# Two-layer dilated attention and GeGLU on one core: exponentials in a PSUM bank of their own, one-bank projection tiles, and a new order table

## The chip, the cores and the metric

The kernel runs on one core of a Trainium2 chip. A core has a matrix engine (TensorE, "PE" in the profile, with its weight loads shown apart as "PEld"), a vector engine (VectorE, "DVE"), a scalar engine (ScalarE, "ACT"), a general engine (GpSimd, "POOL") and an engine that here only issues transfers (SyncE, "SP"). PE writes its products into PSUM, 128 partitions of 16 KB, which this kernel cuts into eight banks of 2 KB (512 float32 columns). The metric is the device time of one execution in microseconds. The time before is the median of three runs, 1265.81 us (1263.17 to 1267.76).

## What is computed

Two layers, each an attention block and a feed-forward block, applied twice to the same weights. The attention looks back at eight positions two apart; positions of one parity see only their own parity.

```python
def _A_ref(x, wqkv, wo):                      # S=2048, D=512, H=32 heads of Dh=16
    W, dil = 8, 2
    q, k, v = split of (x @ wqkv)
    idx = pos[:, None] - (jnp.arange(W) * dil)[None, :]
    logits = einsum("bhsd,bhswd->bhsw", q, k[idx]) * Dh ** -0.5   # -1e9 where idx < 0
    attn = softmax(logits)
    return einsum("bhsw,bhswd->bhsd", attn, v[idx]).reshape(B, S, D) @ wo

def _B_ref(x, w_gate, w_up, w_down):          # F=1792
    return (gelu(x @ w_gate) * (x @ w_up)) @ w_down

x = A_x
x = x + _A_ref(layernorm(x), A_wqkv, A_wo)
x = x + _B_ref(layernorm(x), B_w_gate, B_w_up, B_w_down)
x = x + _A_ref(layernorm(x), A_wqkv, A_wo)
x = x + _B_ref(layernorm(x), B_w_gate, B_w_up, B_w_down)
```

## The kernel before

**Tiling.** The sequence is split by parity and then into chunks of 256 positions (J = 2 tiles of 128), so that a layer has eight chunks and the kernel sixteen. Every matrix is held as a high and a low float16 half, and every product is three passes (high by high, high by low, low by high) that add up in PSUM.

**Stages of a chunk.** (1) Its input is normalised, split and transposed, and projected to query, key and value: for each of the two tiles two halves of the heads, 12 products of 512 columns and 12 of 256 each (line 1047). ACT moves a half out of PSUM (line 1067, staging tile `sc`), and SP stores it to DRAM (`qkvd`). (2) SP loads the windows back (`q`, `kv`), and DVE does the attention: product (line 1131), sum over the head (1140), maximum (1162), subtraction (1167); ACT takes the exponential into PSUM (1172); DVE sums it (1177), inverts (1181), scales it in place (1186), multiplies with the values (1198) and sums (1210). This goes by two groups of heads. (3) The result `o` is split by ACT and POOL (`hl`), transposed by a transfer (`ot`), and PE multiplies it with `w_o` (line 1010 through the helper `passes`); DVE adds it to the residual `x` (1248). (4) The sum is normalised (ACT 858, POOL 934 to 948, ACT 999), split and transposed to `bx`. (5) The feed-forward runs over 14 columns of `w_g` and `w_u` in seven pairs: 48 products of 256 columns a pair (line 1010), the gelu on ACT (1302), gate times up on DVE (1310), sums of blocks on POOL (1321 to 1323), the split on ACT (1331) and POOL (1336, tiles `gh`, and the spare ends of `w_g` and `w_u`, which the profile then names), and 21 down products (line 1345) that add up in the tiles `pd` over the seven pairs. The down product is a fast one of seven blocks (numbered 1 to 7) in place of eight, put together by six DVE sums (line 1374).

**What sets the order.** Nothing is ordered by hand. `Graph.plan` runs all instructions through a list scheduler with estimated durations: of the instructions that can start soonest on an engine it takes the one with the lowest priority number. The priorities are sums of entries of the table `AT`. A tile in PSUM or SBUF is leased from a pool, and an instruction waits in the plan until a slot is free. The program is then emitted in that order, each engine works through its own queue in order, and the waits between engines are added by the tile framework when the program is built. The plan takes two pools for independent, even where their tiles lie in one bank.

**PSUM before.** Two tiles `pg` of two banks; `pds` of four, two and two blocks of 256 columns, so of two banks (profile name pd_121), one bank (pd_122) and one bank (pd_123). Block 1 of the down product is the first half of the last bank, and the exponentials `pe` (pool `P_pe`) are its second half. Until the first down product, pd_121 serves as a third `pg` and pd_122 as the tile `pt` for transposes; the lines `retire` take them away. A pair's four products (gate and up of both columns) share one two-bank `pg`, and so do a half of a projection (768 columns) and both tiles of the `w_o` product.

```python
pds = [ps.tile([P, n, HD], F32, name=f"pd{i}") for i, n in enumerate((4, 2, 2))]
P_pg = Pool("pg", [ps.tile([P, 2, 512], F32, name=f"pg{i}") for i in range(2)]
            + [pds[0].rearrange("p (b m) c -> p b (m c)", b=2)], fifo=False)
P_pe = Pool("pe", [pds[2][:, 1].rearrange("p (j h w) -> p j h w", j=JM, h=AT["ng"] * HPG)])
```

## Time and profile before

| | |
|---|---|
| median of three runs | 1265.81 us (1263.17 to 1267.76) |
| the profiled execution's own time | 1266.16 us |
| its span, first to last instruction | 1264.4 us |
| busy of the span: PE, DVE, POOL, ACT | 95%, 74%, 56%, 42% |
| mean granted PE clock | 0.986 of full |
| products on PE | 9722 |

The span is what the views of the trace describe; the execution's own time is 1.76 us longer. An engine that is busy 95% of the span leaves 62 us, and the question for each microsecond of it is what ended it. Times of the trace are counted from the span's start; "idle before" is the time an engine stood still in front of an instruction, with the instruction or transfer that ended it behind the arrow.

### The profile page before, as it was taken

What the parts mean: (1) busy time and instruction counts of PE and PEld (TensorE: products, weight loads), DVE (VectorE), ACT (ScalarE), POOL (GpSimd) and SP (SyncE); (2) the same over time, 40 slices, a digit from 0 to 9 for tenths busy, and PEclk for the clock granted to TensorE, in tenths of its full rate; (3) what the DMA queues carried; (4) which work ended last, traced back from release to release, by engine and by line L of the source; (5) the groups of instructions that cost most, each with busy time, mean ns of one, the idle gap of its engine ahead of it and who ended that gap; (6) DMA issues with size and microseconds to landing.
All of it is one profiled execution on the core that took longest, in us unless ns stands there. A gap on an engine that the chain in (4) does not pass through costs nothing.

```text
span 1264.4 us, 23933 instructions
## 1 busy us (share of the span) xinstructions
PE 1202.5 (95%) x9722; PEld 954.3 (75%) x9722; DVE 934.4 (74%) x972; ACT 535.6 (42%) x851; POOL 703.7 (56%) x839
## 2 busy tenths in 40 slices
PE   3799989999989999999999999999999999999997
PEld 1455558887878888885778868778788888788886
DVE  7999987788779697717869877676979796578121
ACT  5887633434343534423443333434343534333321
POOL 3323527556575867562285837557565646456543
PEclk7999999999999999999999999999999999999999
DMA  9886893244535434606933454352436343253100
GB/s 350 281 240 188 231 232 106 90 138 138 148 109 153 140 96 155 169 8 192 223 100 108 138 156 137 113 165 87 146 107 168 107 145 78 73 158 63 55 18 18
DMA packets 195790, 174.75 MB, mean 138 GB/s; under 512 B 101904, under 2 KB 162656, under 8 KB 195680
## 3 DMA queue, kind: packets, MB, share of 16 engines
q1 hardware_dynamic: 195680, 173.23, 47.0%
q8 instruction: 76, 1.25, 0.4%
q14 instruction: 34, 0.28, 0.1%
HBM read 115.87 MB, written 33.73 MB: 118 GB/s over the span
## 4 chain that ended last, share of the span: by engine, by line
PE 57%; DVE 13%; POOL 11%; DMA 10%; issue 4%; ACT 3%; SPq 2%; POOLq 0%; ACTq 0%; DVEq 0%
PE pg L1010 36%; PE pd L1345 14%; PE pg L1047 6%; DMA bx<-hl 3%; POOL hl L965 3%; DVE prod L1198 3%; DVE o L1210 2%; DMA ot<-hl 1%; DMA xa<-xs 1%; POOL sc L1321 1%; DVE prod L1131 1%; DVE lg L1140 1%; DMA xs<-x 1%; POOL nw L937 1%; POOL sc L1322 1%
## 5 line engine op out<-in xcount | busy, mean ns | idle before, releaser
L1010 PE MATMUL pg<-bx,w_g 128*128 128x256 f16 x2664 | 328.4, 273 | 1.1 <-DMA bx<-hl 0.7
L1010 PE MATMUL pg<-bx,w_u 128*128 128x256 f16 x2664 | 327.3, 273 | 0.0
L1010 PEld LDWEIGHTS <-w_g 128*128 128x128 f16 x2688 | 263.6, 98 | 37.9 <-DMA bx<-hl 4.7
L1010 PEld LDWEIGHTS <-w_u 128*128 128x128 f16 x2688 | 263.8, 98 | 31.3
L1047 PEld LDWEIGHTS <-ax 128*128 128x128 f16 x1536 | 150.7, 98 | 110.6 <-issue 8.0
L1047 PE MATMUL pg<-w_q,ax 128*128 128x256 f16 (+1 forms) x1320 | 222.8, 328 | 3.0 <-DMA ax<-hl 2.0
L1310 DVE SCALAR_TENSOR_TENSOR sc<-pg,small,sc 128x512 f32<-128x512 f32 (+1 forms) x127 | 85.0, 679 | 145.3 <-ACT sc L1302 139.9
L1321 POOL TENSOR_TENSOR sc<-sc 128x256 f32<-128x256 f32 x112 | 102.3, 913 | 138.3 <-DVE sc L1310 138.0
L1198 DVE TENSOR_TENSOR prod<-kv,pd 128x1024 f32<-128x1024 f32 x128 | 152.3, 1217 | 22.5 <-PE pd L1345 21.4
L1131 DVE TENSOR_TENSOR prod<-kv,q 128x2048 f32<-128x2048 f32 x64 | 160.0, 2500 | 9.6 <-DMA kv<-qkvd 7.2
L1210 DVE TENSOR_REDUCE o<-prod 128x256 f32<-128x2048 f32 x64 | 146.0, 2281 | 17.3 <-POOL hl L965 14.5
L1140 DVE TENSOR_REDUCE lg<-prod 128x128 f32<-128x2048 f32 x64 | 145.8, 2279 | 1.0
L1302 ACT ACTIVATE sc<-pg,small 128x512 f32<-128x512 f32 (+1 forms) x127 | 78.5, 631 | 122.4 <-PE pg L1010 109.6
L965 POOL TENSOR_TENSOR hl<-o,hl 128x256 f16<-128x256 f32 x64 | 44.7, 699 | 133.8 <-ACT hl L961 133.8
L1345 PE MATMUL pd<-w_d,gh 128*128 128x256 f16 x798 | 96.0, 276 | 6.6 <-ACT pd L1172 3.4
L1345 PE MATMUL pd<-w_d,w_u 128*128 128x256 f16 x777 | 92.2, 273 | 7.6 <-ACT pd L1172 6.5
L1336 POOL TENSOR_TENSOR gh<-sc,gh 128x896 f16<-128x896 f32 x38 | 79.7, 2098 | 27.5 <-ACT gh L1331 25.6
L1345 PE MATMUL pd<-w_d,w_g 128*128 128x256 f16 x777 | 91.9, 273 | 2.5 <-ACT pd L1172 2.5
L1336 POOL TENSOR_TENSOR w_g<-sc,w_g 128x896 f16<-128x896 f32 x37 | 77.3, 2088 | 29.1 <-ACT w_g L1331 28.0
L1345 PEld LDWEIGHTS <-gh 128*128 128x128 f16 x798 | 79.0, 99 | 17.9 <-issue 7.5
L1345 PEld LDWEIGHTS <-w_u 128*128 128x128 f16 x777 | 76.0, 98 | 17.7 <-issue 8.7
L1336 POOL TENSOR_TENSOR w_u<-sc,w_u 128x896 f16<-128x896 f32 x37 | 75.3, 2036 | 24.6 <-ACT w_u L1331 24.4
(126 smaller groups left out, 1381.0 us busy)
## 6 DMA issues: line engine op xcount, KB each, us to landing
kv<-qkvd SPq DMA_DIRECT2D x128, 576.0 KB, 3.7
qkvd<-sc SPq DMA_DIRECT2D x64, 384.0 KB, 3.2
q<-qkvd SPq DMA_DIRECT2D x64, 128.0 KB, 3.5
x<-in_A_x_dram SPq DMA_DIRECT2D x9, 512.0 KB, 5.9
xs<-x SPq DMA_DIRECT2D x8, 512.0 KB, 3.0
xa<-xs SPq DMA_DIRECT2D x16, 256.0 KB, 6.0
x<-xs SPq DMA_DIRECT2D x8, 512.0 KB, 4.6
xa<-in_A_x_dram SPq DMA_DIRECT2D x14, 256.0 KB, 4.7
```

Source lines behind the costliest of these rows:

```text
L965: "POOL", t_pool(n), lambda: nc.gpsimd.tensor_sub(lo(), src(), hi()),
L1010: nc.tensor.matmul(pt, a, b, start=i == 0, stop=i == n - 1)
L1047: nc.tensor.matmul(pt[:, lo:hi], a[:, i // 2, kt], part(h * KT + kt)[:, lo:hi], start=(i, kt) == (0, 0), stop=(i, kt) == (2, KT - 1),)
L1131: nc.vector.tensor_mul(prod, win, q.tile().unsqueeze(2).to_broadcast([P, J, W, P]))
L1140: lambda lgv=lgv, heads=heads: nc.vector.tensor_reduce(lgv()[:, :, heads].rearrange("p j h w -> p j w h"), prod.rearrange("p j w (h d) -> ...
L1198: nc.vector.tensor_mul(paired[:, j].rearrange("p q (h d) t -> p q t h d", d=DH), win, by.unsqueeze(4).to_broadcast([P, W // 2, 2, HPG, DH]),)
L1210: lambda o=o: nc.vector.tensor_reduce(o.tile(), paired.rearrange("p j q c t -> p j c q t"), axis=AX.XY, op=ALU.add),
L1302: lambda sel=sel, h=h, pg=pg, g_of=g_of: nc.scalar.activation(g_of()[:, sel], pg.tile()[:, sel, 0:N], AF.Gelu_apprx_tanh, scale=cst["s_gat ...
L1310: lambda sel=sel, h=h, pg=pg, g_of=g_of: nc.vector.scalar_tensor_tensor(g_of()[:, sel], pg.tile()[:, sel, JM * P : JM * P + N], cst["c_up" ...
L1321: tt(b[:, 4:6], b[:, 0:2], b[:, 3:4].to_broadcast([P, 2, P]), op=ALU.add)
L1336: lambda blocks=blocks, gh_of=gh_of: nc.gpsimd.tensor_sub(gh_of()[:, 1], blocks(), gh_of()[:, 0]),
L1345: nc.tensor.matmul(pds_[PD_AT[m][0]].tile()[:, PD_AT[m][1]], gh_of()[:, a, G_AT[m]], wd_of(u, m, b), start=u == 0 and n == 0 and PD_AT[m][ ...
```

## The change

**Banks.** The exponentials get a tile `pe` of one bank that nothing else uses. The accumulators `pds` become four one-bank tiles of two blocks (profile names pd_121 to pd_124), with blocks 4 and 3, 5 and 2, 7 and 6, and 1 alone. For the projections three one-bank `pg` tiles are left (pg_125 to pg_127). Until the first down products, three of the accumulators serve as further `pg` and the third as `pt`.

**Projections.** A half of the query, key and value projection takes two leases, one for its 512 columns and one for its 256, and ACT moves it out in two instructions (line 1076) in place of one. The `w_o` product takes a one-bank tile for each of the two tiles of the chunk. A feed-forward pair puts both its gates in one bank and both its ups in another, in the order gate, gate, up, up, where it was gate, up, gate, up; the gelu waits for the first bank only, gate times up for the gelu and the second bank.

**Down products.** The first and last pair of a chunk, whose 21 down products are placed apart, are cut into four pieces by bank and no longer into three. The six sums are the same six, in another sequence.

**Order.** Almost every entry of `AT` has a new value, and so the plan lays the whole program out anew. The number and the shapes of PE's products are the same.

```diff
-    lq0=-6564.99, lq1=-5227.41, lf0=-588.11, lo=-978.21, lf1=-509.71, ld=28.41, pq0=-2827.04, pq1=4080.31,
+    lq0=-6024.71, lq1=-3848.17, lf0=-1122.81, lo=-1504.86, lf1=-880.86, ld=-724.89, pq0=-2261.26, pq1=1109.7,
...
-PD_AT = {5: (0, 0), 4: (0, 1), 3: (0, 2), 2: (0, 3), 7: (1, 0), 6: (1, 1), 1: (2, 0)}
+PD_AT = {4: (0, 0), 3: (0, 1), 5: (1, 0), 2: (1, 1), 7: (2, 0), 6: (2, 1), 1: (3, 0)}
...
-    pds = [ps.tile([P, n, HD], F32, name=f"pd{i}") for i, n in enumerate((4, 2, 2))]
+    pds = [ps.tile([P, 2, HD], F32, name=f"pd{i}") for i in range(4)]
+    banks = lambda *ts: [t.rearrange("p m c -> p (m c)") for t in ts]
     P_pg = Pool(
-        "pg", [ps.tile([P, 2, 512], F32, name=f"pg{i}") for i in range(2)]
-        + [pds[0].rearrange("p (b m) c -> p b (m c)", b=2)], fifo=False,
+        "pg", [ps.tile([P, 512], F32, name=f"pg{i}") for i in range(3)] + banks(pds[0], pds[1], pds[3]),
+        fifo=False,
     )
-    P_pt = Pool("pt", [pds[1].rearrange("p m c -> p (m c)")], fifo=False)
+    P_pt = Pool("pt", banks(pds[2]), fifo=False)
     P_pd = [Pool(f"pd{i}", [t]) for i, t in enumerate(pds)]
-    P_pe = Pool("pe", [pds[2][:, 1].rearrange("p (j h w) -> p j h w", j=JM, h=AT["ng"] * HPG)])
+    P_pe = Pool("pe", [ps.tile([P, JM, AT["ng"] * HPG, W], F32, name="pe")])
...
-                pg, stg = Lease(P_pg), Lease(P_sc)
+                pgs, stg = [Lease(P_pg) for _ in range(2)], Lease(P_sc)
                 ax = axs[j]
                 staged = lambda stg=stg: stg.tile()[:, 0 : 3 * HH * P]
 
-                def project(ps, h=h, pg=pg, ax=ax):
-                    pt = pg.tile().rearrange("p b c -> p (b c)")
+                cuts = ((0, 512), (512, 768))
+
+                def project(ps, cs, h=h, pgs=pgs, ax=ax):
                     a = ax.tile()
-                    for lo, hi in ((0, 512), (512, 768)):
+                    for n in cs:
+                        lo, hi = cuts[n]
                         for i, kt in ps:
                             part = w_q.lo if i == 1 else w_q.hi
                             nc.tensor.matmul(
-                                pt[:, lo:hi], a[:, i // 2, kt], part(h * KT + kt)[:, lo:hi],
+                                pgs[n].tile()[:, 0 : hi - lo], a[:, i // 2, kt], part(h * KT + kt)[:, lo:hi],
                                 start=(i, kt) == (0, 0), stop=(i, kt) == (2, KT - 1),
                             )
...
+                if l + c + j == 0:
+                    parts = [([p], (n,)) for p in every for n in range(2)]
+                else:
+                    parts = [(every, (n,)) for n in range(2)]
+                for k, (ps, cs) in enumerate(parts):
...
+                        r=[(ax, 0), *need], w=[(pgs[n], 0) for n in cs],
+                        get=[pgs[n] for n in cs] if ps[0] == (0, 0) else [],
+                        prio=prio + AT["proj"] + AT["half"] * h + AT["row"] * j + 0.01 * k, urgent=len(ps) == 1,
...
-                g.add(
-                    "ACT", t_act(768),
-                    lambda pg=pg, staged=staged: nc.scalar.activation(
-                        staged(),
-                        pg.tile().rearrange("p b c -> p (b c)")[:, 0:768],
-                        AF.Copy, scale=2.0**LQ,
-                    ),
-                    r=[(pg, 0)], w=[(stg, 0)], get=[stg], prio=prio - 3000,
-                )
+                for n, (lo, hi) in enumerate(cuts):
+                    g.add(
+                        "ACT", t_act(hi - lo),
+                        lambda n=n, lo=lo, hi=hi, pgs=pgs, staged=staged: nc.scalar.activation(
+                            staged()[:, lo:hi], pgs[n].tile()[:, 0 : hi - lo], AF.Copy, scale=2.0**LQ,
+                        ),
+                        r=[(pgs[n], 0)], w=[(stg, n)], get=[] if n else [stg], prio=prio - 3000,
...
+        for j in range(J):
+            pw = Lease(P_pg)
...
+                "PE", 12 * t_mm(512), project,
+                r=[*((ot, hg) for hg in range(HG)), *(("o", k) for k in range(KT))], w=[(pw, 0)],
+                get=[pw], prio=T - 200,
...
-            pg, gt, gh = Lease(P_pg), Lease(P_sc), Lease(P_gh)
+            pgs, gt, gh = [Lease(P_pg) for _ in range(2)], Lease(P_sc), Lease(P_gh)
             g_of = lambda gt=gt: gt.tile()[:, 0 : 2 * N].rearrange("p (f n) -> p f n", f=2)
             blocks = lambda gt=gt: gt.tile().rearrange("p (m c) -> p m c", m=7)
             gh_of = lambda gh=gh: gh.tile().rearrange("p (a m c) -> p a m c", a=2, m=7)
             fs = (2 * u, 2 * u + 1)
             hs = sorted({f // FH for f in fs})
-            weights = [(key, h * KT + k) for key in "gu" for h in hs for k in range(KT)]
-
-            def gate_up(pg=pg, fs=fs):
-                b = bx.tile()[:, 0:J]
-                for i, f in enumerate(fs):
-                    for n, w in enumerate((w_g, w_u)):
-                        pt = pg.tile()[:, i, n * JM * P : n * JM * P + N]
+
+            for n, (key, w) in enumerate((("g", w_g), ("u", w_u))):
+                def columns(pg=pgs[n], fs=fs, w=w):
+                    b = bx.tile()[:, 0:J]
+                    for i, f in enumerate(fs):
                         passes(
-                            pt.rearrange("p (j c) -> p j c", j=J),
+                            pg.tile()[:, i * N : (i + 1) * N].rearrange("p (j c) -> p j c", j=J),
                             [(wf_of(w, kt, f, True), b[:, :, 0, kt]) for kt in range(KT)]
                             + [(wf_of(w, kt, f, True), b[:, :, 1, kt]) for kt in range(KT)]
                             + [(wf_of(w, kt, f, False), b[:, :, 0, kt]) for kt in range(KT)],
                         )
 
-            g.add(
-                "PE", 48 * max(t_mm(N), 0.06), gate_up, r=[*((bx, j) for j in range(J)), *weights],
-                w=[(pg, 0)], get=[pg], prio=T + AT["gu"] * J * u,
-            )
-            gate = lambda i, pg=pg: pg.tile()[:, i, 0:N]
-            up = lambda i, pg=pg: pg.tile()[:, i, JM * P : JM * P + N]
+                g.add(
+                    "PE", 24 * t_mm(N), columns,
+                    r=[*((bx, j) for j in range(J)), *((key, h * KT + k) for h in hs for k in range(KT))],
+                    w=[(pgs[n], 0)], get=[pgs[n]], prio=T + AT["gu"] * J * u + 0.01 * n,
+                )
+            part = lambda n, sel, pgs=pgs: pgs[n].tile().rearrange("p (f c) -> p f c", f=2)[:, sel]
             both = fs[0] // FH == fs[1] // FH
             ev = T - 3000 + u
             for i in [None] if both else [0, 1]:
...
                 n = N * (2 if both else 1)
                 g.add(
                     "ACT", t_act(n, 1),
-                    lambda sel=sel, h=h, pg=pg, g_of=g_of: nc.scalar.activation(
-                        g_of()[:, sel], pg.tile()[:, sel, 0:N], AF.Gelu_apprx_tanh,
-                        scale=cst["s_gate", h],
+                    lambda sel=sel, h=h, part=part, g_of=g_of: nc.scalar.activation(
+                        g_of()[:, sel], part(0, sel), AF.Gelu_apprx_tanh, scale=cst["s_gate", h],
                     ),
-                    r=[(pg, 0), ("c_f", h)], w=[(gt, i)], get=[] if i else [gt, gh] if hold else [gt], prio=ev, table="gelu",
+                    r=[(pgs[0], 0), ("c_f", h)], w=[(gt, i)], get=[] if i else [gt, gh] if hold else [gt], prio=ev, table="gelu",
                 )
                 g.add(
                     "DVE", t_dvp(n),
-                    lambda sel=sel, h=h, pg=pg, g_of=g_of: nc.vector.scalar_tensor_tensor(
-                        g_of()[:, sel], pg.tile()[:, sel, JM * P : JM * P + N],
-                        cst["c_up", h], g_of()[:, sel], op0=ALU.mult, op1=ALU.mult,
+                    lambda sel=sel, h=h, part=part, g_of=g_of: nc.vector.scalar_tensor_tensor(
+                        g_of()[:, sel], part(1, sel), cst["c_up", h], g_of()[:, sel], op0=ALU.mult, op1=ALU.mult,
                     ),
-                    r=[(pg, 0)], w=[(gt, i)], prio=ev,
+                    r=[(pgs[1], 0)], w=[(gt, i)], prio=ev,
...
-            order = [5, 4, 3, 2, 7, 6, 1]
+            order = [4, 3, 5, 2, 7, 6, 1]
             lag = AT["late_end"] if last else AT["late"]
-            for ms in [order[:4], order[4:6], order[6:]] if u in (0, NU - 1) else [order]:
+            for ms in [order[k : k + 2] for k in range(0, 7, 2)] if u in (0, NU - 1) else [order]:
                 i = PD_AT[ms[0]][0]
...
-            step = b - a
-            return t[:, a : b + 1 : step] if step else t[:, a : a + 1].to_broadcast([P, 2, HD])
+            r = t[:, a]
+            return bass.AP(r.tensor, r.offset, [r.ap[0], [(b - a) * HD, 2], [1, HD]])
 
         parts = lambda: xl.tile()[:, 0:J].rearrange("p j (d c) -> p (j d) c", d=2)
         for to, of, sign in (
-            ((1, 2), (5, 4), 1), ((0, 3), (4, 3), 1), ((0, 3), (5, 2), -1), ((1, 2), (3, 2), 1),
+            ((0, 3), (4, 3), 1), ((2, 1), (4, 3), 1), ((1, 2), (5, 2), 1), ((0, 3), (5, 2), -1),
...
-    for q, i in ((P_pg, 2), (P_pt, 0)):
+    for q, i in ((P_pg, 3), (P_pg, 4), (P_pt, 0), (P_pg, 5)):
...
-    retire[1].order.extend(turns)
+    retire[2].order.extend(turns)
```

Three places show what moves. The first is PE at the down products of the last pair of chunk 0 (`gh` is the split tile of the pair, with PE's waits in brackets). Before, they follow two whole pairs of the next chunk:

```order
L1010 MATMUL pg_125<-bx_95,w_u 128x256
...
L1345 MATMUL pd_121<-w_d,gh 128x256
...
L1345 LDWEIGHTS gh [waits Pool_49]
...
L1345 MATMUL pd_122<-w_d,gh 128x256
...
L1345 MATMUL pd_123<-w_d,gh 128x256 [waits Activation_49]
...
L1345 LDWEIGHTS w_g
```

In the changed kernel:

```order
L1011 MATMUL pg_127<-bx_96,w_g 128x256
L1346 LDWEIGHTS gh [waits Activation_49]
L1346 MATMUL pd_121<-w_d,gh 128x256
...
L1346 LDWEIGHTS gh [waits Pool_49]
...
L1346 MATMUL pd_122<-w_d,gh 128x256
...
L1346 MATMUL pd_123<-w_d,gh 128x256
...
L1346 MATMUL pd_124<-w_d,gh 128x256
...
L1011 MATMUL pg_126<-bx_96,w_g 128x256 [waits DVE_49]
```

The product into the last bank loses its wait for ACT (pd_123 before held block 1 and the exponentials; pd_124 holds block 1 alone), and the down products stand between the gates and the ups of another pair. Over the whole program 62 down products into pd_123 carry a wait for ACT or DVE before; of the changed kernel's 2352 down products two carry a wait on the product itself, one for DVE and one for a transfer.

The second is DVE where chunk 0 adds its `w_o` product to the residual `x_91`, ahead of the first feed-forward. Before:

```order
L1131 TENSOR_TENSOR prod<-kv_104,q_107 128x2048
L730 TENSOR_TENSOR w_d<-bx_96,w_d 128x7x128
L1140 TENSOR_REDUCE lg_108<-prod 128x2x8x8
L1248 SCALAR_TENSOR_TENSOR x_91<-pd_121,small,x_91 128x512 x2
L730 TENSOR_TENSOR w_d<-sc_100,w_d 128x7x128
```

In the changed kernel:

```order
L1254 SCALAR_TENSOR_TENSOR x_91<-pd_121,small,x_91 128x512
L731 TENSOR_TENSOR w_d<-bx_96,w_d 128x7x128
L1254 SCALAR_TENSOR_TENSOR x_91<-pg_126,small,x_91 128x512
L731 TENSOR_TENSOR w_d<-sc_102,w_d 128x7x128
L1138 TENSOR_TENSOR prod<-kv_104,q_107 128x2048
L1147 TENSOR_REDUCE lg_108<-prod 128x2x8x8
```

The two additions now stand ahead of one attention product and one reduction of the next chunk, and each has a tile of its own. On PE the `w_o` product of chunk 0 moves the other way: 27 of the 32 projection halves of layer 0 stand ahead of it before, 28 in the changed kernel; in both all 32 stand ahead of the first gate.

The third is SP at the two transposes that bring the normalised chunk 0 to `bx_95`. Before:

```order
L1078 DMA qkvd_64<-sc_100 128x6x128
L970 DMA_TRANSPOSE bx_95<-hl_98 128x8x128
L970 DMA_TRANSPOSE bx_95<-hl_99 128x8x128
L1078 DMA qkvd_64<-sc_102 128x6x128
L1108 DMA q_107<-qkvd_64 128x256
```

In the changed kernel:

```order
L1115 DMA kv_104<-qkvd_64 128x1152
L971 DMA_TRANSPOSE bx_95<-hl_99 128x8x128
L1085 DMA qkvd_64<-sc_101 128x6x128
L971 DMA_TRANSPOSE bx_95<-hl_98 128x8x128
L1085 DMA qkvd_64<-sc_100 128x6x128
```

The second transpose now stands behind a store of a projection half, which waits for both of ACT's moves of that half.

49 lines of the change are left out of this document (20 added, 29 removed).

## The prediction

> **What bounds the kernel now.** I read the page's busy times first, then the waits of PE, then PE's timeline at the longest of them, then the waits of DVE.
>
> ```profile
> span 1264.4 us, 23933 instructions
> PE 1202.5 (95%) x9722; PEld 954.3 (75%) x9722; DVE 934.4 (74%) x972; ACT 535.6 (42%) x851; POOL 703.7 (56%) x839
> ```
>
> PE is busy 95% of the span, and it is the bound. What it must do follows from the time of its groups when nothing stops them:
>
> ```profile
> 944.89 3.90 PE pg L1047 x24
> ...
> 1214.93 20.96 PE pg L1010 x192
> ...
> 1243.42 12.79 PE pd L1345 x117
> ```
>
> In the chain that ended last, the second and third row give 0.109 us for 256 columns, the first 3.90 us for half a projection. So the 112 pairs take 112 x 5.24 = 587 us, the 112 groups of 21 down products 112 x 2.29 = 257, the 64 projection halves 250, the 16 `w_o` products (24 of 512 columns, 5.24 us) 84: 1178 us. That floor is the same in the changed kernel. Of it 130 us (32 halves and one `w_o`) stand ahead of the first gate in both orders, 1048 us behind it.
>
> ```profile
> 183.49 1.95 PE L1010 MATMUL pd<-bx,w_g 128*128 128x256 f16 x12 [3.46 <-DMA bx<-hl]
> ...
> 1256.23 4.37 DVE L1374 SCALAR_TENSOR_TENSOR x<-pd,small,x 128x512 f32<-128x512 f32 x6 [11.25 <-PE pd L1345]
> ```
>
> The first gate starts at 183.5, so unhindered PE would end at 1231.5; it ends at about 1256.2, and the last sums and the store take the remaining 8.2 us. The 24.7 us between are waits and a slow clock. These are the waits of PE behind 180 us:
>
> ```profile
> PE pd L1345 <- ACT pd L1172: 12.4, 10, 3.5
> ...
> PE pd L1345 <- DVE prod L1198: 4.4, 4, 1.9
> ...
> PE pd L1010 <- DMA bx<-hl: 3.5, 1, 3.5
> ...
> PE pg L1047 <- ACT sc L1067: 1.0, 1, 1.0
> ...
> PE pg L1010 <- DMA bx<-hl: 0.7, 1, 0.7
> ...
> PE pg L1010 <- DVE sc L1310: 0.3, 1, 0.3
> ```
>
> 16.8 of the 22.3 us are one thing: a down product (L1345) waits for an exponential (L1172) or for a product that reads the exponentials (L1198). No data goes from either to a down product. What they have in common is the bank pd_123. PE's timeline shows it:
>
> ```profile
> 251.25 2.13 PE L1345 MATMUL pd<-w_d,gh 128*128 128x256 f16 x18
> 255.91 0.75 PE L1345 MATMUL pd<-w_d,gh 128*128 128x256 f16 x3 [2.54 <-ACT pd L1172]
> 256.45 2.77 PE L1010 MATMUL pg<-bx,w_g 128*128 128x256 f16 x12
> ...
> 371.92 0.70 PE L1345 MATMUL pd<-w_d,w_u 128*128 128x256 f16 x3 [3.46 <-ACT pd L1172]
> ```
>
> Eighteen of the 21 products run, the three of block 1 wait. The gates behind them then take 2.77 us where twelve take 1.31. The windows name the cause:
>
> ```profile
> 180.00:200.00 20.00, 16.55 (x138) 14.12 (x137) 15.32 (x14) 8.49 (x11) 5.49 (x7) 0.91 0.64 168
> 240.00:260.00 20.00, 17.46 (x146) 14.88 (x144) 19.13 (x19) 6.58 (x9) 12.21 (x14) 0.91 0.35 110
> 360.00:380.00 20.00, 16.54 (x130) 13.38 (x128) 13.36 (x14) 9.65 (x15) 13.77 (x17) 0.91 0.35 100
> ```
>
> In the three stretches with PE's longest waits (3.46, 2.54, 3.46 us) the granted clock is 0.91, which is 20 x 0.09 = 1.8 us lost in each. The same bank holds DVE up too:
>
> ```profile
> DVE mx L1177 <- PE pd L1345: 29.5, 10, 7.7
> ...
> DVE prod L1198 <- PE pd L1345: 21.4, 13, 3.7
> ...
> DVE pd L1186 <- PE pd L1345: 5.8, 5, 1.9
> ```
>
> That is 56.7 us in which the softmax stands behind down products it has nothing to do with. So the 24.7 us behind the first gate are accounted for: 18.8 of waits (22.3 without the gate's own 3.5) and 3 x 1.8 of clock.
>
> **The change part by part.**
>
> *A bank for the exponentials.* In the changed order none of the softmax instructions waits for PE, and a down product has a wait of its own twice. So the 16.8 us go, and with two of the three long waits two clock losses, 2 x 1.8 = 3.6. DVE's 56.7 us are not added: they only keep the chain of attention from taking over. What is late next on PE is the data: `bx` and the lower halves of `gh`, below. The Trainium skill, "TensorE: Matmul & The Clock Gate", section "HAM oscillation — how this bites in real kernels", warns of idle gaps of PE above about 3.4 us. By it the 2.54 us gap would have kept the clock, and this term would be 1.8 instead of 3.6; the window 240 to 260 shows the loss, so the trace differs.
>
> *The first gate.* Chunk 0 goes from `w_o` to `bx` by a chain that PE waits for:
>
> ```profile
> 155.19 5.34 PE L1010 MATMUL pd<-w_o,ot 128*128 128x512 f16 x24
> 161.12 1.40 DVE L1248 SCALAR_TENSOR_TENSOR x<-pd,small,x 128x512 f32<-128x512 f32 x2
> ...
> 175.27 5.93 SPq L970 DMA_TRANSPOSE bx<-hl  x2
> ```
>
> The changed order has one more projection half ahead of `w_o`, so it starts 3.9 us later, at 159.1. DVE comes 4.6 us earlier (one product and one reduction are moved behind), and waits. Its second addition can start when PE is done, 164.4, and ends at 165.2, against 162.5: 2.7 us later, and `bx` and the first gate with it, while PE's own work ahead ends where it did. On SP the second transpose now stands behind a store, behind which the attention's loads are queued too; the store needs a half that PE ends at about 176.1, so the transpose could go out at 178 and not 176.9, which lies inside the 2.7. I take 2.7; the lower bound is 0, since two DVE splits are moved behind those of `w_q`, for which PE waits early on, and the upper 5, where both delays add and a little more:
>
> ```profile
> PE pd L1047 <- DVE w_q L524: 3.0, 2, 2.6
> ```
>
> *More and smaller moves by ACT.*
>
> ```profile
> L1067 ACT ACTIVATE sc<-pg 128x768 f32<-128x768 f32 x55 | 44.3, 806 | 53.6 <-PE pg L1047 38.2 <-DMA qkvd<-sc 10.6 <-POOL w_g L1336 2.0
> ...
> L858 ACT ACTIVATE sc<-x 128x512 f32<-128x512 f32 x32 | 20.1, 628 | 33.5 <-DVE x L1248 21.1 <-issue 4.3 <-POOL w_u L1336 3.8
> ...
> L1172 ACT ACTIVATE pd<-lg 128x256 f32<-128x256 f32 x8 | 3.1, 388 | 2.7 <-DVE prod L1198 2.6
> ```
>
> 512 and 256 columns take 628 + 388 = 1016 ns where 768 took 806: 64 x 0.21 = 13.4 us more on ACT. It is busy 42%, and a bank that was due in 3.9 us still is; cost 0. Without that cover the halves ahead of the first gate would bring 32 x 0.21 = 6.7 us.
>
> *Three banks for the rotation.* A gate's or up's bank is due again after two other banks, 5.24 us of products, if nothing stands between; that was so with two tiles of a pair. But in the changed order 66 of 172 such returns come after no more than these 5.24 us, before 11 of 80. And the down products stand nearer to their pair: at least 6.9 us of products behind its last up, and 13 of 112 no more than 9.5; before at least 10.5. What must fit in is gate times up, three sums, the split and its lower half:
>
> ```profile
> L1310 DVE SCALAR_TENSOR_TENSOR sc<-pg,small,sc 128x512 f32<-128x512 f32 x95 | 70.9, 746 | 117.9 <-ACT sc L1302 112.4 <-POOL nw L941 5.0
> ...
> L1321 POOL TENSOR_TENSOR sc<-sc 128x256 f32<-128x256 f32 x112 | 102.3, 913 | 138.3 <-DVE sc L1310 138.0
> L1323 POOL TENSOR_TENSOR sc<-sc 128x256 f32<-128x256 f32 x112 | 83.6, 747 | 8.8
> L1336 POOL TENSOR_TENSOR gh<-sc,gh 128x896 f16<-128x896 f32 x38 | 79.7, 2098 | 27.5 <-ACT gh L1331 25.6 <-ACT nw L867 1.7
> ```
>
> With some 0.6 us for the middle sum and 0.9 for the split that is 6.0 us when nobody is held up (the gelu is done by then, it waits for the gates alone). DVE carries instructions of 2.3 to 2.5 us and POOL of 2.1, so a chain can come late. Bounds: 0, and all 66 returns late by half a microsecond, 33. The nearest rows are the 1.3 us that PE waited for a `pg` before; the places with no slack are six times as many, which gives 8, and the gelu starts earlier: I take 6.
>
> *The tail.* The first two sums need six products and not twelve: 6 x 0.109 = 0.65 us sooner.
>
> *Sum.* 1264.4 - 16.8 - 3.6 + 2.7 + 6 - 0.65 = 1252 us of span. The profiled execution's own time, 1266.16, is 1.76 longer than its span and 0.35 above the median of the runs, so the run is 1252 + 1.4 = **1253.5**, 12 us or 1.0% less than 1265.81.
>
> **The rivals.**
>
> *The attention sets the pace of layer 0.* Until 473 us, when its sixth chunk is through, DVE feeds PE with little to spare:
>
> ```profile
> 184.00:473.00 289.00, 279.24 (x2353) 232.40 (x2352) 227.90 (x212) 117.25 (x186) 183.18 (x210) 0.98 0.44 127
> ```
> ```profile
> DVE mx L1177 <- PE pd L1345: 15.4, 4, 7.7
> ...
> DVE prod L1198 <- PE pd L1345: 4.3, 4, 1.5
> DVE pd L1186 <- PE pd L1345: 3.0, 3, 1.4
> ```
> ```profile
> 398.79 2.29 DVE L1210 TENSOR_REDUCE o<-prod 128x256 f32<-128x2048 f32 x1
> ...
> 410.43 1.89 PE L1010 MATMUL pg<-w_o,ot 128*128 128x512 f16 x8
> ```
>  If chunks come no sooner, what PE saves there (2.54 + 3.46 of the timeline, 2.7 in two shorter waits, 3.6 of clock, together 12.3) comes back as waits for `ot`, and 8.1 remain: 1264.4 - 8.1 + 2.7 - 0.65 + 1.4, about 1260. For it: DVE is busy 79% there (227.9 of 289), and PE takes a chunk's `w_o` 9.3 us after DVE's last reduction, with a split, a transpose and their queues in between. Against: DVE itself waits 22.7 us for PE's down products in the same stretch, and is relieved of it. Chance 0.17.
>
> *The change gives back what it takes.* The waits go, and PE waits for banks: each of the 66 tight returns late by 0.3 us makes 20, on the 1246 of the sum without new waits. About 1267, no change. For it: the count of tight returns. Against: 1.3 us in all before, and the gelu and gate times up now each wait for less. Chance 0.12.
>
> *Slower: the lower halves come late.* The 13 down products at 9.5 us or less have 3.5 us of room over the bare chain. One long DVE instruction ahead (2.3 us) fits in, two (4.8) do not, and POOL's own 2.1 on top makes a lag of 3.4 us. Nine of the 13 so late are 31 us: 1246 + 31 + 1.4, about 1278. It decides from the point at which the queues ahead of the chain hold more than 3.5 us at most of these places. For it: the 79% of DVE above. Against: before, no down product waited for POOL at all. Chance 0.13.
>
> **How the numbers follow.** Forecast 0.58, the rivals 0.17, 0.12 and 0.13. A measurement of this kernel tells a difference from none at about 0.3%, 3.8 us: below 1262.0 is faster, above 1269.6 slower. Forecast and first rival lie below (0.75), the second within, the third above; 0.01 of the first rival, which ends near the edge, goes to no change, and 0.02 of the second, where banks are later still, to slower. The forecast's own range is 1243 to 1262: no new wait, none of the 2 us of small ones kept and the first gate at 183.5 on the one side, 12 us of new waits and the gate 5 late on the other. It is widened to 1268 to hold the second rival, and down to 1239 for a first gate that gains its 3.46 us of waiting.
>
> **What would show it.** The waits of PE would hold no line of L1346 for the exponential (L1179) or its reader (L1205), and those of DVE none of L1184 for PE; the windows after 240 us no clock of 0.91. The first gate would stand at 186. New lines of PE behind 190 us, for `pg` or the lower halves, would sum to some 6 us. The prediction is wrong if those lines exceed 15 us, or if `w_o` waits for `ot` in the first six chunks.

## The result, and the profile after

The changed kernel takes 1246.2 us, the median of four runs (1244.98 to 1248.89), against 1265.95 in four runs of the kernel before (1263.17 to 1267.76): a ratio of 0.9849, with a 95% interval of 0.9825 to 0.9873. The forecast was 1253.5, so the direction and the mechanism held and the gain is 7.3 us larger. The profiled execution took 1246.04 us, its span 1244.3.

The page's busy times:

```profile
PE 1200.8 (97%) x9722; PEld 954.1 (77%) x9722; DVE 935.5 (75%) x972; ACT 542.0 (44%) x911; POOL 690.2 (55%) x839
```

PE does the same 9722 products in the same busy time within 2 us; of the 62 us it did not work, 43.5 are left. The chain of work that ended last, by engine, is now 84% PE (it was 57% PE, 13% DVE, 11% POOL and 10% DMA before).

The waits of PE from the first gate on (engine, line waited in, what it waited for; total us, times, longest), all of them:

```profile
PE pg L1011 <- DMA bx<-hl: 5.1, 2, 4.6
PE pg L1050 <- ACT sc L1076: 1.4, 1, 1.4
PE pg L1011 <- DMA ot<-hl: 0.5, 2, 0.3
```

No down product (L1346) waits for anything. Behind the first gate, whose own wait is 4.58, four waits of together 2.4 us are left of 17 of 18.8. PE's timeline at the first gate, and at its last group of down products:

```profile
186.11 4.45 PE L1011 MATMUL pg<-bx,w_g 128*128 128x256 f16 x24 [4.58 <-DMA bx<-hl]
190.39 2.78 PE L1011 MATMUL pd<-bx,w_u 128*128 128x256 f16 x24
...
1234.97 2.46 PE L1346 MATMUL pd<-w_d,gh 128*128 128x256 f16 x21
```

The first 24 products take 4.45 us, the next 24 2.78: one clock loss of 1.67 us is left, behind the first gate. The windows at the places of the other two (us, busy us and count of each engine, then granted clock) are back at full clock:

```profile
180.00:200.00 20.00, 15.42 (x126) 12.92 (x125) 18.25 (x18) 8.12 (x11) 6.64 (x6) 0.91 0.70 192
240.00:260.00 20.00, 20.00 (x186) 17.94 (x184) 18.39 (x18) 7.16 (x9) 9.85 (x9) 1.00 0.36 114
360.00:380.00 20.00, 20.00 (x174) 16.77 (x173) 11.88 (x12) 3.65 (x6) 8.14 (x11) 1.00 0.36 107
```

The waits of DVE, and its longest group in the kernel before:

```profile
DVE sc L1312 <- PE pg L1011: 143.1, 53, 6.9
...
DVE mx L1184 <- ACT pe L1179: 16.1, 12, 4.5
```
```profile
DVE sc L1310 <- ACT sc L1302: 143.1, 53, 11.4
```

The softmax waits for ACT's exponential alone and no longer for PE. Gate times up (L1310, now L1312) used to wait 143.1 us for the gelu, and now waits as long for the ups themselves: the gelu, which needs the gates alone, is mostly done when the ups arrive (10.6 us of waits for it are left).

**Where the time came from.** The last group of down products of the kernel before, in PE's timeline:

```profile
1254.72 2.46 PE L1345 MATMUL pd<-w_d,gh 128*128 128x256 f16 x21
```

From the first gate to the start of that group it was 1254.72 - 183.49 = 1071.2 us, and is 1234.97 - 186.11 = 1048.9, so 22.4 less. Second profiles of both kernels, shown below, give 1071.0 and 1049.9, so 21.1 less.

In the first pair the waits give 18.8 - 2.4 = 16.4. Two clock losses give 3.3: in the kernel before, 27 products from 255.91 on take 4.61 us where 0.109 each is 2.95, and 45 from 371.92 on take 6.58 where it is 4.91, so 1.67 us for each. The remaining 2 us are the stops themselves. In the prediction's rows 18 products take 2.13 us, which is 18 x 0.109 and 0.16 more: the last product before a stop is counted in full, although the next one would have started behind it after 0.109. So each stop costs 0.16 us beyond the idle time the profile shows, and 13 stops fewer are 2.1. The sum is 21.8, and 0.6 of the 22.4 stays open. In the second pair the waits give 18.7 - 3.2 = 15.5, the clock 3.3 and 15 stops fewer 2.4, together 21.2.

PE's busy time agrees: between these marks it falls from 1052.1 to 1046.4 us in the first pair. The page's total hides this, because ahead of the first gate it rises there from 147.9 to 151.9 us; in the second pair that part is 150.4 and 150.0, so the rise is not in both pairs.

### The profile page after: what moved, and what is told of

Read it like the earlier page. It is cut to its first block, busy times and chain, and to the rows that moved or that the text cites. A ratio compares the mean times of both kernels' runs of the same rounds, so it can differ in the third digit from the quotient of the medians.

```text
span 1244.3 us, 24043 instructions
## 1 busy us (share of the span) xinstructions
PE 1200.8 (97%) x9722; PEld 954.1 (77%) x9722; DVE 935.5 (75%) x972; ACT 542.0 (44%) x911; POOL 690.2 (55%) x839
## 4 chain that ended last, share of the span: by engine, by line
PE 84%; DMA 5%; DVE 4%; POOL 3%; issue 2%; ACT 1%; SPq 0%; POOLq 0%; DVEq 0%; ACTq 0%
PE pg L1011 51%; PE pd L1346 20%; PE pg L1050 9%; PE pd L1050 3%; DMA ax<-hl 2%; POOL hl L966 1%; DMA bx<-hl 1%; DMA xa<-xs 1%; DMA ot<-hl 1%; PE pd L1011 1%; DMA kv<-qkvd 1%; DVE prod L1138 1%; DMA w_d<-in_A_wqkv_dram 1%; POOL nw L938 0%; DVE w_q L525 0%
## 5 line engine op out<-in xcount | busy, mean ns | idle before, releaser
L1011 PE MATMUL pg<-bx,w_g 128*128 128x256 f16 x2664 | 310.6, 273 | 5.1 <-DMA bx<-hl 5.1
L1011 PE MATMUL pg<-bx,w_u 128*128 128x256 f16 x2664 | 309.0, 273 | 0.0
L1011 PEld LDWEIGHTS <-w_u 128*128 128x128 f16 x2688 | 263.0, 98 | 30.6
L1050 PE MATMUL pg<-w_q,ax 128*128 128x512 f16 (+1 forms) x1152 | 203.0, 334 | 6.3 <-DVE w_q L525 4.2
L1312 DVE SCALAR_TENSOR_TENSOR sc<-pg,small,sc 128x512 f32<-128x512 f32 (+1 forms) x127 | 85.1, 680 | 157.7 <-PE pg L1011 143.1
L1322 POOL TENSOR_TENSOR sc<-sc 128x256 f32<-128x256 f32 x112 | 100.4, 896 | 127.0 <-DVE sc L1312 120.9
L1138 DVE TENSOR_TENSOR prod<-kv,q 128x2048 f32<-128x2048 f32 x64 | 152.6, 2385 | 7.8 <-DMA kv<-qkvd 7.1
L1205 DVE TENSOR_TENSOR prod<-kv,pe 128x1024 f32<-128x1024 f32 x128 | 152.6, 1216 | 1.4
L966 POOL TENSOR_TENSOR hl<-o,hl 128x256 f16<-128x256 f32 x64 | 59.2, 926 | 109.9 <-ACT hl L962 109.5
L1375 DVE SCALAR_TENSOR_TENSOR x<-pd,small,x 128x512 f32<-128x512 f32 x96 | 70.5, 743 | 32.9 <-PE pd L1346 31.4
L1346 PE MATMUL pd<-w_d,gh 128*128 128x256 f16 x798 | 93.5, 273 | 0.0
L1337 POOL TENSOR_TENSOR gh<-sc,gh 128x896 f16<-128x896 f32 x38 | 76.1, 2003 | 29.8 <-ACT gh L1332 29.6
L1346 PE MATMUL pd<-w_d,w_u 128*128 128x256 f16 x777 | 91.0, 273 | 0.0
L1346 PE MATMUL pd<-w_d,w_g 128*128 128x256 f16 x777 | 90.9, 273 | 0.0
L1324 POOL TENSOR_TENSOR sc<-sc 128x256 f32<-128x256 f32 x112 | 83.6, 747 | 8.8
```

Of the source, the lines that this page charges most:

```text
L1011: nc.tensor.matmul(pt, a, b, start=i == 0, stop=i == n - 1)
L1050: nc.tensor.matmul(pgs[n].tile()[:, 0 : hi - lo], a[:, i // 2, kt], part(h * KT + kt)[:, lo:hi], start=(i, kt) == (0, 0), stop=(i, kt) == ...
L1138: nc.vector.tensor_mul(prod, win, q.tile().unsqueeze(2).to_broadcast([P, J, W, P]))
L1205: nc.vector.tensor_mul(paired[:, j].rearrange("p q (h d) t -> p q t h d", d=DH), win, by.unsqueeze(4).to_broadcast([P, W // 2, 2, HPG, DH]),)
L1312: lambda sel=sel, h=h, part=part, g_of=g_of: nc.vector.scalar_tensor_tensor(g_of()[:, sel], part(1, sel), cst["c_up", h], g_of()[:, sel], ...
L1322: tt(b[:, 4:6], b[:, 0:2], b[:, 3:4].to_broadcast([P, 2, P]), op=ALU.add)
```

## The experiments

Each ratio below is to runs of the kernel before on the same chip; their medians lay between 1265.05 and 1267.5 us.

**1. The shared bank alone put back.** Tiles, split moves and order are the changed kernel's; the exponentials lie beside block 1 again.

```diff
-        "pg", [... for i in range(3)] + banks(pds[0], pds[1], pds[3]),
+        "pg", [... for i in range(3)] + banks(pds[0], pds[1]) + [ps.tile([P, 512], F32, name="spare")],
-    P_pe = Pool("pe", [ps.tile([P, JM, AT["ng"] * HPG, W], F32, name="pe")])
+    P_pe = Pool("pe", [pds[3][:, 1].rearrange("p (j h w) -> p j h w", j=JM, h=AT["ng"] * HPG)])
```

> The changed kernel with one thing put back: the exponentials lie again in the second half of a bank, beside block 1 of the down product (pd_124); the bank that this frees serves as a startup tile. The order of all instructions is that of the changed kernel. Theory (the shared bank is what cost PE time): waits of the down products for the exponential (L1179) or its readers (L1205) come back, and DVE's waits in the softmax for down products too; 15 to 25 us slower than the changed kernel, 1261 to 1271 us. Rival (the new order is what gained, the bank is incidental): within 4 us of the changed kernel, 1243 to 1250, since the new order would keep the two users of the bank apart.

Measured: 1263.65 us median of 10 runs; to the kernel before (1266.95) a ratio of 0.9981 [0.9965, 0.9997]. Against the changed kernel's 0.9849 this is 1.3% or some 17 us slower, and nearly all of the gain is gone. Its waits of PE behind the first gate, and two of DVE's:

```profile
PE pd L1346 <- DVE prod L1205: 9.3, 10, 1.5
PE pg L1011 <- DMA bx<-hl: 4.0, 3, 1.7
...
PE pd L1346 <- ACT pd L1179: 0.8, 1, 0.8
```
```profile
DVE prod L1205 <- PE pd L1346: 14.9, 13, 3.4
DVE pd L1193 <- PE pd L1346: 12.3, 7, 3.8
```

The theory holds: the false waits are back in both directions. Directly they are 10.1 us on PE; a further 5.6 us above the 2.4 of the changed kernel are waits for `bx`, `ot`, a gelu and a lower half that come late, which fits a DVE that is held up, though no chain from one to the other was followed. All waits behind the first gate sum to 18.1 us in 19 stops, so 15.7 us and 15 stops (2.4 us) more than after. From the first gate to the last down group this kernel takes 1252.20 - 184.53 = 1067.7 us, 18.3 more than the 1049.4 of the changed kernel's two profiles, which is 15.7 + 2.4 and little else.

The new order lessens the sharing but does not evade it. For the softmax PE waits 10.1 us here against 16.8 in the kernel before, never longer than 1.5 us, and from 190 to 1240 us the granted clock is 1.00. So part of those waits and both clock losses of the kernel before go with the new order and tiles already, and the rest of this run's price is late data and stops.

**2 and 3. The two order tables exchanged.** The changed kernel with the table `AT` of before, and the kernel before with the table of the changed one.

```diff
-    lq0=-6024.71, lq1=-3848.17, lf0=-1122.81, lo=-1504.86, lf1=-880.86, ld=-724.89, pq0=-2261.26, pq1=1109.7,
+    lq0=-6564.99, lq1=-5227.41, lf0=-588.11, lo=-978.21, lf1=-509.71, ld=28.41, pq0=-2827.04, pq1=4080.31,
...
```

> The changed kernel with the order table of before: banks, tiles and split moves are new, the numbers that set the order are old. Theory (the banks are what gained): no wait of a down product for the softmax, so most of the gain stays; the table was not made for one-bank tiles, so some waits for pg or for the lower halves of gh: 1246 to 1256 us. Rival (the table is what gained): 1262 us or more.

> The kernel before with the order table of the changed kernel: shared bank and two-bank tiles as before. Theory (the banks are what gained): waits of the down products for the softmax stay at 15 us or more, 1262 to 1280 us. Rival (the table is what gained): 1244 to 1254 us.

Measured: the new banks with the old table 1309.13 us, a ratio of 1.0344 [1.0327, 1.0361]; the old banks with the new table 1270.28, 1.0042 [1.0027, 1.0056]. For the first, the expectation that most of the gain stays was wrong: it is 63 us slower than the changed kernel. The time lies in the rival's range (1262 us or more), but the second run shows that the table alone is not what gained either. The waits of PE in the first run, from 180 us on, the longest groups:

```profile
PE pg L1011 <- DMA bx<-hl: 21.5, 4, 11.3
PE pg L1011 <- ACT sc L1305: 10.3, 14, 2.1
PE pg L1011 <- DMA ot<-hl: 5.7, 5, 2.0
PE pd L1346 <- POOL gh L1337: 3.8, 3, 1.6
PE pg L1011 <- DVE sc L1312: 3.1, 4, 1.4
PE pg L1050 <- ACT sc L1305: 3.0, 1, 3.0
PE pg L1050 <- ACT sc L1076: 1.8, 4, 0.8
PE pg L1011 <- DVE x L1254: 1.5, 3, 0.8
```

Here is the rotation's price that the prediction feared: 19.7 us of waits for a bank that ACT or DVE has not yet emptied (row 2 and the last four), and chunks whose input comes up to 11.3 us late. With a table laid out for three one-bank tiles the same tiles cost 1.4 us.

The second run's time lies where it was expected, but not for the reason given: its down products wait 9.6 us for the softmax (the two rows below and 1.1 for the maximum), and not 15 or more. Its first gate, its last down group, and these waits:

```profile
198.52 2.72 PE L1010 MATMUL pg<-bx,w_g 128*128 128x256 f16 x12 [8.10 <-DMA bx<-hl]
...
1257.79 2.46 PE L1345 MATMUL pd<-w_d,gh 128*128 128x256 f16 x21
```
```profile
PE pd L1345 <- DVE prod L1198: 5.0, 7, 1.5
PE pd L1345 <- ACT pd L1172: 3.5, 4, 1.4
```

Between those marks it takes 1059.3 us, some 12 less than the kernel before, but its first gate stands 10 to 15 us later than in that kernel's two profiles (183.49 and 188.28). So the new table gains behind the first gate with the old banks too and loses as much ahead of it, which the time alone hides. Against this run the changed kernel is 9.9 us shorter behind the first gate (1059.3 less 1049.4) and reaches it 12 to 14 us sooner. Why the startup is so late with the old banks was not followed, and it is one profile.

So the bank and the table are not two gains that add up. With the new table the own bank is worth some 17 us; with the old one the new banks lose 42.

**4. The exponentials out of PSUM, order as before.** The kernel before, its order kept on every engine, with the exponentials in 1 KB of SBUF that the zeros and the identity of the start leave free.

```diff
-    ident = sb.tile([P, P], F32, name="ident")
+    ident = (pes := sb.tile([P, 2 * P], F32, name="pe"))[:, P:]
-    P_pe = Pool("pe", [pds[2][:, 1].rearrange("p (j h w) -> p j h w", j=JM, h=AT["ng"] * HPG)])
+    P_pe = Pool("pe", [pes.rearrange("p (j h w) -> p j h w", j=JM, h=AT["ng"] * HPG)])
-    zeros = sb.tile([P, P], F32, name="zeros")
+    zeros = pes[:, 0:P]
```

> The kernel before with the exponentials in SBUF (in 1 KB that the zeros and the identity matrix of the start leave free), nothing else: same order on every engine, two-bank tiles, one move per projection half. Theory: PE loses the 16.8 us of bank waits and two of three clock losses, 3.6 us, and what it meets instead is at most 3 us: 1245 to 1250 us, as fast as the changed kernel, so that tiles, split and table add nothing. Rival one (attention sets the pace of layer 0): some 8 us come off and the rest comes back as waits of w_o for ot before 473 us, 1256 to 1261 us. Rival two (the table is needed): 1262 us or more.

Measured: 1290.43 us, a ratio of 1.0195 [1.0171, 1.0220], slower than every expectation. As a test of the shared bank it fails, because it changes something else. Groups of DVE and POOL in this kernel (line, operation, tiles, count, busy us, mean ns of one, idle before):

```profile
L1198 DVE TENSOR_TENSOR prod<-kv,pe 128x1024 f32<-128x1024 f32 x128 | 201.3, 1602 | 1.1
...
L1321 POOL TENSOR_TENSOR sc<-sc 128x256 f32<-128x256 f32 x112 | 123.4, 1102 | 94.1 <-DVE sc L1310 94.0
```

and the first in the kernel before:

```profile
L1198 DVE TENSOR_TENSOR prod<-kv,pd 128x1024 f32<-128x1024 f32 x128 | 152.3, 1217 | 22.5 <-PE pd L1345 21.4
```

The waits for PE are gone (21.4 to nothing), but the product of values and exponentials takes 1602 ns and not 1217, and POOL's first sum 1102 and not 913. DVE is busy 994.6 us and not 934.4, POOL 778.1 and not 703.7. The Trainium skill, "SBUF — State Buffer", section "SBUF: two separate sides", says that a DVE instruction with two SBUF inputs and a GpSimd instruction that reads SBUF exclude each other on a port pair. The trace agrees: both engines lengthen when the second input leaves PSUM, and in the rows below where they meet. They do not show the port itself. DVE's timeline of this kernel, and POOL's beside it:

```profile
511.71 1.23 DVE L1198 TENSOR_TENSOR prod<-kv,pe 128x1024 f32<-128x1024 f32 x1
...
517.09 4.47 DVE L1198 TENSOR_TENSOR prod<-kv,pe 128x1024 f32<-128x1024 f32 x2
```
```profile
513.68 1.64 POOL L1321 TENSOR_TENSOR sc<-sc 128x256 f32<-128x256 f32 x1 [4.24 <-DVE sc L1310]
...
517.61 2.86 POOL L1336 TENSOR_TENSOR w_g<-sc,w_g 128x896 f16<-128x896 f32 x1
```

While POOL stands idle the product takes 1.23 us, as it did with PSUM; beside POOL's split two of them take 4.47. POOL's sum, which has a median of 0.73 us, takes 1.64 where it starts just after such a product (one runs from 513.51 to 514.73). Over the whole run the product takes 1204 ns at the least and 2932 at the most, and 1186 to 1251 in the kernel before.

DVE is now busy 77% of the span, and what PE waits for most is:

```profile
PE pg L1010 <- DVE sc L1310: 7.5, 6, 2.2
PE pg L1010 <- DMA ot<-hl: 7.0, 8, 1.4
```

These are late attention (`ot`, eight times) and late gate times up. It is not the prediction's first rival, which has attention set the pace up to 473 us: of the 7.0 us for `ot` 0.7 lie there, and the rest behind 700 us. The bank of its own has to be a PSUM bank, and the eight banks of the kernel before were all taken: the two-bank tiles had to go for it.

**5. ACT's split doubled.** Each of the two moves of a projection half becomes two.

```diff
-nc.scalar.activation(staged()[:, lo:hi], pgs[n].tile()[:, 0 : hi - lo], AF.Copy, scale=2.0**LQ)
+[nc.scalar.activation(
+    staged()[:, lo + c : lo + c + (hi - lo) // 2], pgs[n].tile()[:, c : c + (hi - lo) // 2], AF.Copy, scale=2.0**LQ,
+) for c in (0, (hi - lo) // 2)][-1]
```

> The changed kernel with each of ACT's two moves of a projection half cut into two again (four moves a half, 128 instructions more on ACT), order otherwise the same. Theory (ACT is far from the bound, so that the split costs nothing): ACT's busy time rises by 20 to 30 us, the time stays within 2 us of the changed kernel, 1244 to 1249. Rival (each move holds a bank that PE waits for): at least the 32 halves ahead of the first gate show it, 6 us or more, 1252 or above.

Measured: 1246.5 us, 0.9849 [0.9820, 0.9877], the same ratio as the changed kernel. ACT's busy time rises by 7.3 us (549.3 against 542.0) and not by the 20 to 30 expected, since a move of half the columns is that much shorter: two of 256 columns take 2 x 381 ns where one of 512 took 594, two of 128 take 2 x 279 for 381. The test is so a weak one, but hardly any of the 7.3 us reaches PE, whose one wait for such a move goes from 1.4 to 1.9 us. That agrees with the prediction's cost of 0 for the first split.

**6 and 7. How much room the banks have.** Each gelu done twice, then four times.

```diff
-nc.scalar.activation(g_of()[:, sel], part(0, sel), AF.Gelu_apprx_tanh, scale=cst["s_gate", h])
+[nc.scalar.activation(g_of()[:, sel], part(0, sel), AF.Gelu_apprx_tanh, scale=cst["s_gate", h]) for _ in range(2)][-1]
```

> The changed kernel with each gelu done twice (the same result is written again; 127 instructions and 79 us more on ACT), so that each gate's bank and all that follows it in the pair comes 0.63 us later. Theory (the new waits were small because the banks and lower halves have room of a microsecond or more nearly everywhere): waits of PE for pg and gh grow by 1 to 6 us, 1247 to 1253 us. Rival (the 66 returns of a bank after 5.24 us of products have no room, and the new order only just fits): two thirds of 66 x 0.63 and more, 1270 us or above.

> As the last, with each gelu done four times: 1.9 us later in each pair, ACT busy some 63%. Theory (room of some 3 us between a gate's bank and its next use): the room is used up at the tight places, PE's waits for pg and for the lower halves grow to 15 to 60 us, 1260 to 1305 us; each further microsecond of delay costs more than the first. Rival one (no room at all): 66 x 1.9 and more, 1370 us or above. Rival two (room of several microseconds): under 1256 us.

Measured: twice 1249.3 us (0.9870 [0.9840, 0.9900]), four times 1299.55 (1.0266 [1.0234, 1.0298]). PE's waits behind the first gate with two, and with four (there without two rows of 1.9 and 1.1 us for ACT):

```profile
PE pg L1011 <- DMA bx<-hl: 1.7, 2, 1.2
PE pg L1050 <- ACT sc L1076: 1.6, 1, 1.6
PE pd L1346 <- POOL w_g L1337: 0.7, 1, 0.7
PE pg L1011 <- DMA ot<-hl: 0.3, 1, 0.3
```
```profile
PE pg L1011 <- ACT sc L1305: 16.9, 10, 3.6
PE pg L1011 <- DMA ot<-hl: 8.5, 6, 3.4
PE pg L1011 <- DMA bx<-hl: 5.8, 3, 2.9
PE pd L1346 <- POOL gh L1337: 5.0, 5, 1.6
...
PE pd L1346 <- POOL w_g L1337: 1.6, 1, 1.6
...
PE pd L1346 <- POOL w_u L1337: 0.9, 2, 0.5
```

With 0.63 us more in each pair PE waits 4.3 us in place of 2.4, and nowhere for a gate's bank. With 1.9 us more it waits 41.7, ten times and 16.9 us for a gate's bank, eight times and 7.5 us for a lower half. So the gates' banks have more than 0.6 us of room everywhere, and at some ten places less than the later gelu takes; the count of tight returns told where the edge is, not how far away. That a gelu holds ACT from its other work too (`ot` and `bx` are late) is part of the second figure, and the two are not told apart.

**8 and 9. The wait of the first gate filled.** First the last projection piece ahead of the gate is computed four times; then, in its place, 36 products that nobody uses follow it, in the first gate's bank.

```diff
+                    made.append(cs)
-                    for n in cs:
+                    for n in cs * (4 if len(made) == 108 else 1):
```
```diff
-                def columns(pg=pgs[n], fs=fs, w=w):
+                def columns(pg=pgs[n], fs=fs, w=w, fill=36 * (l + c + u + n == 0)):
...
+                    for _ in range(fill):
+                        nc.tensor.matmul(pg.tile()[:, 0:N], ident16, w_o.hi(0)[:, 0:N], start=True, stop=True)
```

> The changed kernel with the last 12 projection products ahead of the first gate computed four times in place of once (36 products of 256 columns more, 3.9 us, the last result counts), so that PE's wait of 4.58 us for bx shrinks to about 0.7 us; order otherwise the same. Theory (the half clock behind a long wait of PE comes from the wait): the first gate stays at 186 us, its 24 products take 2.8 us in place of 4.45, the clock of 180 to 200 us rises from 0.91 to 1.0, and the end comes 1.7 us earlier: 1243 to 1246 us. Rival (the slow products behind a wait have another cause, such as the data or the weights of the new stage): 24 products stay at 4.4 us, and the time at 1246 or up to 1 us above.

> The changed kernel with 36 products of 256 columns (3.9 us) whose result nobody uses, put into the bank of the first gate just ahead of it, behind the last projection half; order otherwise the same. In the run with the last half computed four times the clock held, but that half's store and the next chunk's attention came 3.9 us later and PE waited 3.3 us more for bx, ot and DVE behind the first gate. Theory (those waits came from the late half, and the clock from the idle time): first gate at 186 us, 24 products in 2.8 us, waits behind it back at some 2.5 us, span 1242 to 1243.5 us, 1.7 us less than the changed kernel, time 1243 to 1246. Rival (an earlier PE meets late data anyway): clock 1.0, but the waits behind the first gate grow by 1.7 us and the span stays at 1244 us or above.

Measured: 1246.67 us (0.9849 [0.9826, 0.9872]) and 1245.95 (0.9841 [0.9819, 0.9862]). PE's timeline at the first gate, of the second of the two:

```profile
179.89 4.09 PE L1284 MATMUL pg<-w_o,ident 128*128 128x256 f16 x36
184.40 2.79 PE L1011 MATMUL pg<-bx,w_g 128*128 128x256 f16 x24 [0.42 <-DMA bx<-hl]
```

The 24 products take 2.79 us and not 4.45, and in the first kernel 2.78: the slow products come with PE's idle time, and not from the data or the weights. The time does not follow. Behind the gate PE then waits 5.7 us in the first kernel and 4.1 in the second, 2.4 before the fill and 3.2 in the second profile of the changed kernel. A saving of 1.7 us and a return of about one lie inside the spread of the runs, so whether the fill gains anything is not settled; neither kernel is measurably faster than the changed one.

**10 and 11. Both kernels again.**

> The changed kernel itself, for a second profile and for times beside the run above: 1244 to 1249 us, the first gate at 185 to 187 us, waits of PE behind it of 2 to 4 us, as in the first profile.

> The kernel before itself, for a second profile. If the first gate's place differs from run to run by as much as between the two profiles of the changed kernel (184.31 and 186.11 us), it will stand anywhere from 182 to 186 us here, and the 2.6 us between the first two profiles is partly chance; if it is fixed by the order, it stands within 0.5 us of 183.5. The waits of down products for the softmax: 15 to 19 us in 12 to 16 waits, as in the first profile; time 1263 to 1270 us.

Measured: the changed kernel 1245.36 us in five runs beside 1267.5 (ratio 0.9832 [0.9815, 0.9850]); the kernel before in its one profiled run 1270.77. The expectations missed in part: the changed kernel's first gate comes earlier than 185, and that of the kernel before at 188.28, outside both ranges given for it; its down products wait 14.9 us for the softmax in 14 waits, just under the 15 to 19, and its one time lies just above 1270. The first gate and the last group of down products in these profiles, of the kernel before and then of the changed kernel:

```profile
188.28 2.72 PE L1010 MATMUL pd<-bx,w_g 128*128 128x256 f16 x12 [4.68 <-DMA bx<-hl]
...
1259.32 2.46 PE L1345 MATMUL pd<-w_d,gh 128*128 128x256 f16 x21
```
```profile
184.31 4.45 PE L1011 MATMUL pg<-bx,w_g 128*128 128x256 f16 x24 [4.68 <-DMA bx<-hl]
...
1234.22 2.46 PE L1346 MATMUL pd<-w_d,gh 128*128 128x256 f16 x21
```

The place of the first gate is not set by the order alone: one program has it at 183.49 and 188.28, the other at 186.11 and 184.31. Four experiments that keep the changed kernel's order ahead of the gate (1, 5, 6 and 7) have it at 184.53, 185.34, 185.18 and 185.96. From the gate to the last down group the second profiles agree with the first (1259.32 - 188.28 = 1071.0, and 1234.22 - 184.31 = 1049.9), so the spread arises in the startup and the gain behind it.

## Why the prediction was right, and where its sizes were off

| term of the sum | predicted, us | measured, us |
|---|---|---|
| waits of down products for the softmax | -16.8 | -16.8 |
| two clock losses | -3.6 | -3.3 |
| first gate | +2.7 | no shift that stands out of the spread of 4.8 |
| small waits kept and new ones | 2.0 kept + 6 | 2.4 together |
| overhead of 13 stops | not in the sum | -2.1 |
| tail | -0.65 | -0.4 |
| ACT's split, on PE | 0 | 0 |

**The bank.** Right, and the first experiment shows it as the cause: with everything else new, sharing the bank again costs some 17 us. But the prediction put all of the 16.8 us and both clock losses down to the bank. With the bank shared and the new table PE waits only 10.1 us for the softmax in the new tiles and 9.6 in the old, and neither loses the clock anywhere behind the slow products of its first gate; so some 7 us of the waits and the 3.3 of clock would have gone with the order alone. What makes the bank worth 17 us all the same is late data and stops beside those 10 us, and the sum held neither. The prediction gave DVE's side no worth in time; with the bank shared, 5.6 of PE's 18.1 us are waits for late data and not for the bank, so that side may have been worth something in the new order.

**The new waits** are the term that was mis-sized, by 5.6 us (8 expected with the small ones, 2.4 found) and most of the 7.3 by which the forecast was too slow. The step at fault is "the places with no slack are six times as many, which gives 8": it multiplied a price by a count of places, 66 of 172 returns against 11 of 80, and took "after no more than 5.24 us of products" for "with no slack". The twofold gelu shows room of more than 0.6 us at all the gates' banks; the ups' banks, which DVE empties, it need not have delayed. The rows of DVE fit that: gate times up seldom stands behind a gelu now, so that a bank is emptied within some 0.7 us (the mean of L1312 is 680 ns) of its last product when DVE stands ready. The fear itself was sound. With the old table the same tiles cost 19.7 us.

**The clock.** Right in mechanism, shown by the two fills, and nearly in size: 1.67 us for each loss and not 1.8. That a wait of 2.54 us loses the clock was read rightly from the window, though not every such wait does.

**The first gate.** The step compared one profile with an order, and its figure cannot be confirmed: 183.5 was the early end of what that program does, since its second profile has 188.28. The forecast for the place, 186, lies among the values seen for the changed order (184.31 to 186.11), but that it did so is partly luck.

**The stops** were missed. Some 2 us went into "busy" in the kernel before, so that a sum over idle times alone is too small by 0.16 us a stop. The prediction's account of the 24.7 us behind the first gate closed without them (18.8 of waits and 5.4 of clock) because it took 1256.2 us for PE's end; the last down group, 2.46 us from 1254.72 on, ends at 1257.2.

**The rivals.** The attention does not set the pace of layer 0: PE waits for `ot` 0.5 us in all. Even with 60 us more on DVE and 74 on POOL, in the fourth experiment, PE waits for `ot` only 0.7 us up to 473 us, though 6.3 behind 700. The change gives nothing back, and no lower half is late; with 1.9 us more in each pair both happen (16.9 us for banks, 7.5 for lower halves), so the room between the forecast and these rivals was real but under 2 us at some places.

## What to carry to other kernels

Where one line waits for another without any data passing between them, look for the bank they share, and count the idle time, a further 0.16 us for each stop, the clock behind those of some 2 us and more, and the time of the other engine that waits in return. A new layout of banks and the order made for it are one change: try them in all four combinations before crediting either. The count of places where a buffer returns quickly is no price; lengthening the instruction that empties it by a known amount measures the room, as far as the other work of that engine is not held up with it.
